# Attention and two expert layers on one core: the first batch's gate moves from TensorE's products into VectorE's row-maximum pass

## The chip, the cores and the metric

The kernel runs on one core of one Trainium2 chip. The metric is the device time of one execution in microseconds (us), the median of several executions. The engines have their usual names in the rows: PE is TensorE's matrix products and PEld its weight loads, DVE is VectorE, ACT is ScalarE, POOL is GpSimd, SP is the queue that issues most DMAs.

## The reference

The reference is a chain of three blocks in single precision. Only the first concerns the change: a causal attention over 4 batches, 8 heads, 576 positions and a head size of 64, whose scores get a gate from a running sum.

```python
scores = scale * np.matmul(q, k.transpose(0, 1, 3, 2))
s_pos = np.maximum(s, 0.0)
cum = np.cumsum(s_pos, axis=-1)
bias = -(cum[:, :, :, None] - cum[:, :, None, :])
scores = np.where(causal, -1000000000.0, scores + np.minimum(bias, 0.0))
scores = scores - np.max(scores, axis=-1, keepdims=True)
attn = np.exp(scores)
attn = attn / (np.sum(attn, axis=-1, keepdims=True) + 1e-09)
return np.matmul(attn, v).astype(np.float32)
```

Behind it stand a first expert layer (512 to 1024 to 512, softmax, normalization) and a second one (512 to 2048 to 512). The running sum never falls, so the minimum with 0 only acts above the diagonal, which the mask covers anyway. The part of the bias that belongs to the row (`-cum[i]`) is the same for all columns and drops out when the row's maximum is subtracted; only `+cum[j]` is left.

## The kernel before, in words

The 32 pairs of batch and head are worked two heads at a time. A head's rows are cut into five tiles (`SZ` = 128, 128, 128, 96, 96 rows, starting at `ST`), and tile `t` has only the columns up to its own end. Batches 1 to 3 hold q, k and the gate stacked along the contraction and split into high and low parts (`qk`, L615). The first batch is worked otherwise (`prep_whole`, `qk_whole`): q and k of a pair of heads are transposed in full precision (L445), head `j` on the partitions `64 j` to `64 j + 63`, and for every tile TensorE makes four products (L588), for each head one of the gate and one of q and k, which add up in one PSUM bank. The gate's product has contraction 64, of which 4 partitions are set: `gates_at` gives rows 0 to 3 of a zeroed block of `whole_t`, which hold the sum's high and low parts, once as such beside ones and once negated. These rows are made by `gate_rows` at the start: a running sum on VectorE (L283), three more VectorE instructions (L284 to L286), four stores to `rows_d` in DRAM (L290), and one load for each head (L432).

The first batch is worked in two ranges: first tiles 0 and 1 of all four pairs (`a=False`), whose output starts the first expert layer, then tiles 2 to 4 of all four pairs (`a=True`). For each product `tops` (L536) reads the bank and a causal mask, writes the negated score and gives the row's maximum in the same VectorE pass; ScalarE takes the exponential in place (L548); VectorE inverts the sums (L644, L645); GpSimd scales the rows (L649); TensorE transposes them (L683) and multiplies with v (L712). Between these stand the conversions of the expert weights from a 64-bit format: a load of 512 KB by ScalarE's queue (L322), instructions on ScalarE, VectorE (L332, L336, L343) and GpSimd (L352). The first expert layer starts with L799 and L803 (x into high and low parts) and its products L817.

No order is written by hand: the functions add operations to `Plan`, each with an engine, an assumed duration, the keys that it reads and writes, and for a DMA a `lag` until it has landed. `Plan.emit` plays these through and emits each engine's instructions in the order of the starts that come out. Engines run in that order; only real dependencies hold them.

`whole_t[0]` serves pairs 0 and 2, `whole_t[1]` pairs 1 and 3, of both ranges. For pairs 2 and 3 q and k lie in the same tile as the gate (`[:, :2]` and `[:, 2:4]`).

Of the kernel before, what the change touches and what calls it, by code (L numbers as in the profile page):

```python
# [18 lines left out]
NEG = -1.0e30  # L19
# [170 lines left out]
def kernel(ctx, tc, q, k, v, s, w_in, w_out, g_ln, w2_in, w2_out, out):  # L190
# [30 lines left out]
    rows_d = dram.tile([NH, 2, 4, S], F32, name="rows_d")  # L221
    x2_d = dram.tile([P, KDM, NT], F32, name="x2_d")
# [46 lines left out]
    def gate_rows():  # L269
# [3 lines left out]
        one = ap2.tile([P, S], F32, tag="y4", name="one")[:NH]  # L273
        cum = ap2.tile([P, NQ, 2, D], F32, tag="V", name="cum").rearrange("p c j d -> p (c j d)")[:NH, :S]
        pos = ap2.tile([P, PT_COLS], F32, tag="pt", name="pos", bufs=PT).bitcast(F32R)[:NH, : 2 * S]
        neg = ap2.tile([P, PT_COLS], F32, tag="pt", name="neg", bufs=PT).bitcast(F32R)[:NH, : 2 * S]
# [19 lines left out]
        plan.add("SP", 0.45, load, writes=["s"], lag=2.0)  # L296
        plan.add("DVE", 2.2, lambda: nc.vector.memset(one, 1.0), writes=["one"])
        for j in range(2):
            plan.add("POOL", 1.05, lambda j=j: zeros(j), writes=[f"zeros{j}"], new=[(f"stack{j}", 1, f"whole{j}")])
        plan.add("POOL", 0.4, constants)  # L300
# [3 lines left out]
        for i, r, src, key in ((1, 0, both(pos), "c"), (0, 1, both(neg), "c"), (0, 0, ones, "one"), (1, 1, ones, "one")):  # L304
# [228 lines left out]
    def tops(h, t, c0, c1, at, key):  # L533
# [3 lines left out]
            out=ys[h, t][:n, c0:c1], in0=bank(key)[:n, : c1 - c0], in1=mask[:n, 480 + n - w + c0 : 480 + n - w + c1], scale=-1.0, scalar=3.0e38,  # L537
# [20 lines left out]
    def qk_whole(p, t):  # L558
# [21 lines left out]
        def mm(c0, c1, keys):  # L580
            if c0 == 0:
                homes()
            for m in range(2):
                for j in range(2):
                    r = slice(j * D, (j + 1) * D)
                    g, hl = gates_at(p, j), hls[f"HL{p}"][r]
                    a, b = (hl[:, 0, :], hl[:, 1, :]) if m else (g[:, 0, :], g[:, 1, :])
                    nc.tensor.matmul(bank(keys[j])[:n, : c1 - c0], lhsT=a[:, ST[t] : w], rhs=b[:, c0:c1], start=(m == 0), stop=(m == 1))  # L588

        pieces = pieces_of(t)  # L590
        for c0, c1, at in pieces:
# [4 lines left out]
            elif c0 == 0 and t == ts[0]:  # L596
# [808 lines left out]
```

## Time and profile before

| | |
|---|---|
| median of 3 executions | 828.55 us (827.94 to 829.88) |
| profiled execution, first to last instruction | 826.7 us |
| PE busy in it | 800.2 us, 97% |
| DVE, ACT, POOL busy | 540.2 us, 424.0 us, 210.1 us |

The profiled execution has no time of its own beside its span. The median lies 1.85 us above that span and the fastest execution 1.2 us; what is read from the trace is a difference, and is taken from the median as it stands. All four engines work side by side, so their sums don't add up to the span; the engine's share says how much of it could be hidden behind another one.

### The profile page before, as it was taken

Reading aid. Unit: us, or ns where it says so; the run is one execution under the profiler, and the core shown is the slowest. Engines: PE = TensorE matmul, PEld = TensorE weight load, DVE = VectorE, ACT = ScalarE, POOL = GpSimd, SP = SyncE. Lnnn points to the kernel's source line nnn. Section 1 sums busy time; section 2 is a strip of 40 time slices with the busy share of each in tenths; the row PEclk is TensorE's granted clock in tenths of the full one; section 3 lists DMA queues with packets and bytes.
Section 4 is the critical chain, followed back from the end, with each engine's and each line's share of the span. In section 5 each row is a group of like instructions: output and inputs, shape, how many; then the busy total and the mean of one; then the engine's idle time right before and its main releaser. Section 6 shows DMA issues by size and latency. Waiting matters only on the chain.

```text
span 826.7 us, 14172 instructions
## 1 busy us (share of the span) xinstructions
PE 800.2 (97%) x4960; PEld 696.7 (84%) x4960; DVE 540.2 (65%) x1344; ACT 424.0 (51%) x994; POOL 210.1 (25%) x308
## 2 busy tenths in 40 slices
PE   3899999999999999999999999999999999999997
PEld 2655688898898888897999999999998989998996
DVE  3777887756847577648844994648867677455351
ACT  2575777756756566546644763335434335323223
POOL 2563653524632454245420231000000000000000
PEclk9999999999999999999999999999999999999999
DMA  6753586755645564305613679724424443524302
GB/s 167 192 155 105 124 212 142 175 134 130 132 99 137 138 131 99 89 27 172 192 52 111 221 217 355 261 78 135 172 101 145 161 140 134 210 90 147 121 1 76
DMA packets 110726, 117.41 MB, mean 142 GB/s; under 512 B 65248, under 2 KB 89312, under 8 KB 108608
## 3 DMA queue, kind: packets, MB, share of 16 engines
q1 hardware_dynamic: 108352, 108.12, 46.3%
q10 hardware_dynamic: 2304, 8.39, 3.1%
q8 instruction: 39, 0.64, 0.3%
q14 instruction: 31, 0.25, 0.1%
HBM read 68.45 MB, written 26.80 MB: 115 GB/s over the span
## 4 chain that ended last, share of the span: by engine, by line
PE 91%; DVE 4%; DMA 2%; POOL 2%; issue 1%; ACT 0%; POOLq 0%; SPq 0%; DVEq 0%; ACTq 0%
PE bank L1134 24%; PE bank L1270 14%; PE bank L904 12%; PE bank L817 11%; PE bank L1122 8%; PE bank L712 6%; PE bank L615 5%; PE bank L683 5%; PE bank L588 3%; PE bank L883 2%; PE bank L478 1%; DMA whole<-rows_d 1%; DMA rows_d<-neg 1%; POOL y L649 1%; POOL y L631 1%
## 5 line engine op out<-in xcount | busy, mean ns | idle before, releaser
L1134 PE MATMUL bank<-w2o,gb 128*128 128x512 f32 x576 | 137.2, 391 | 0.0
L1134 PEld LDWEIGHTS bank<-w2o,gb 128*128 128x128 f32 x576 | 107.6, 188 | 20.9
L1270 PE MATMUL bank<-xb,ws 128*128 128x384 f32 x672 | 123.8, 336 | 0.0
L1270 PEld LDWEIGHTS bank<-xb,ws 128*128 128x128 f32 x672 | 118.5, 188 | 3.2 <-DVE c L1283 0.3
L536 DVE CUSTOM_DVE_ANT_0 y<-bank,mask 96x288 f32<-96x288 f32 (+4 forms) x168 | 74.6, 467 | 57.0 <-PE bank L615 37.3
L548 ACT ACTIVATE y<-y,nmax 128x256 f32<-128x256 f32 (+4 forms) x140 | 83.5, 598 | 40.9 <-DVE nmax L536 27.7
L1283 DVE TENSOR_TENSOR c<-c,bank 128x384 f32<-128x384 f32 x112 | 60.3, 551 | 63.4 <-PE bank L1270 59.9
L631 POOL TENSOR_SCALAR y<-y,rsum 128x128 f32<-128x128 f32 (+4 forms) x120 | 68.9, 592 | 102.9 <-DVE rsum L627 42.5
L904 PE MATMUL bank<-zh,w_out_h 128*128 128x256 f32 x288 | 82.8, 288 | 0.0
L904 PE MATMUL bank<-zl,w_out_h 128*128 128x256 f32 x288 | 80.9, 281 | 0.0
L904 PE MATMUL bank<-zh,w_out_l 128*128 128x256 f32 x288 | 80.9, 281 | 0.0
L1122 PE MATMUL bank<-xk,wp 128*128 128x384 f32 x320 | 72.0, 337 | 0.0
L1134 PE MATMUL bank<-w2o,gs 128*128 128x512 f32 x288 | 71.7, 393 | 0.0
L1099 ACT ACTIVATE ggb<-c 128x384 f32<-128x384 f32 x64 | 32.7, 523 | 58.2 <-DVE c L1283 56.6
L817 PE MATMUL bank<-w_in_h,xh 128*128 128x512 f32 x144 | 61.4, 426 | 0.8 <-DVE xh L799 0.8
L1134 PEld LDWEIGHTS bank<-w2o,gs 128*128 128x128 f32 x288 | 53.6, 188 | 9.7
L1122 PEld LDWEIGHTS bank<-xk,wp 128*128 128x128 f32 x320 | 57.3, 188 | 1.9
L615 PE MATMUL bank<-stack 128*96 128x288 f32 (+4 forms) x288 | 57.8, 317 | 0.5 <-DMA stack<-rows_d 0.5
L817 PE MATMUL bank<-w_in_h,xl 128*128 128x512 f32 x144 | 57.3, 398 | 0.6 <-POOL xl L803 0.6
L817 PE MATMUL bank<-w_in_l,xh 128*128 128x512 f32 x144 | 57.2, 397 | 0.0
L904 PEld LDWEIGHTS bank<-zh,w_out_h 128*128 128x128 f32 x288 | 54.2, 188 | 1.1 <-DVE zl L890 0.2
L904 PEld LDWEIGHTS bank<-zh,w_out_l 128*128 128x128 f32 x288 | 54.3, 189 | 0.3
(239 smaller groups left out, 1521.6 us busy)
## 6 DMA issues: line engine op xcount, KB each, us to landing
ws<-ws_d SPq DMA_DIRECT2D x8, 1792.0 KB
raw_w2i<-in_moe_w_in_dram SPq DMA_DIRECT2D x16, 512.0 KB
raw_w2o<-in_moe_w_out_dram SPq DMA_DIRECT2D x16, 512.0 KB
ws<-ws_d SPq DMA_DIRECT2D x8, 1024.0 KB
ws_d<-ws SPq DMA_DIRECT2D x16, 512.0 KB
ws_d<-wp SPq DMA_DIRECT2D x24, 256.0 KB
rawq<-in_q_dram SPq DMA_DIRECT2D x32, 144.0 KB
rawk<-in_k_dram SPq DMA_DIRECT2D x32, 144.0 KB
```

The source lines that it names most:

```text
L536: nc.vector.tensor_tensor_reduce(out=ys[h, t][:n, c0:c1], in0=bank(key)[:n, : c1 - c0], in1=mask[:n, 480 + n - w + c0 : 480 + n - w + c1], ...
L548: nc.scalar.activation(out=y[:n], in_=y[:n], func=AF.Exp, bias=nmax[:n, h, t : t + 1], scale=-1.0, accum_out=sums[:n, h, t : t + 1])
L615: nc.tensor.matmul(bank(key)[:n, : c1 - c0], lhsT=ss[:, 2 - 2 * m, ST[t] : w], rhs=ss[:, 3 - 2 * m, c0:c1], start=(m == 0), stop=(m == 1))
L631: nc.gpsimd.tensor_scalar(ys[h, t][:n], ys[h, t][:n], rsum[:n, h, t : t + 1], 1.0, ALU.mult, ALU.mult)
L683: nc.tensor.transpose(bank(key)[: SZ[jj], c : c + SZ[t]], ys[h, t][: SZ[t], ST[jj] : ST[jj] + SZ[jj]], ident[: SZ[t], : SZ[t]])
L712: nc.tensor.matmul(bank(key)[j * D : (j + 1) * D, lo - c0 : c1 - c0], lhsT=vs[v_key(p, a)][:n, jj, j, :], rhs=pts[pt_key(2 * p + j, a)][:n ...
L817: nc.tensor.matmul(bank(key), lhsT=xs[i][m // 2][:, kk, :], rhs=(w_in_l if m == 1 else w_in_h)[:, kk, f * 512 : (f + 1) * 512], start=(kk ...
L904: nc.tensor.matmul(bank(key)[:, : 2 * P], lhsT=w_out_at(w, kk)[:, m * P : (m + 1) * P], rhs=z[:, kk, :], start=(kk == 0 and i == 0), stop= ...
L1122: nc.tensor.matmul(bank(key)[:, :W], lhsT=w2i_at(m, a)[:, c * P : (c + 1) * P], rhs=x[:, b, :], start=(c == 0 and i == 0), stop=(c == KDM ...
L1134: nc.tensor.matmul(bank(key), lhsT=g_t[name][:, i // 2, (t % TRIO) * P : (t % TRIO + 1) * P], rhs=w2o[m][:, i % 2, :], start=(m == 0 and i ...
L1270: nc.tensor.matmul(bank(key)[:, :W], lhsT=ws[bi, k][:, WOP[op], x, kc * P : (kc + 1) * P], rhs=xb[bi, op][:, y, kc, :], start=(kc == 0 and ...
L1283: nc.vector.tensor_add(g_t[to_key], g_t[from_key], bank(key)[:, :W])
```

## The change

In the first batch the gate no longer goes through TensorE. The running sum is stored once (`cum_d`, 72 KB) and for a pair and range one DMA reads the two heads' rows back to all 128 partitions (256 KB for tiles 0 and 1, 576 KB for tiles 2 to 4). GpSimd puts a large negative number above the diagonal of each tile's own block in this copy (`triangle`), and `tops` takes the copy in place of the mask. Since a tile's triangle spoils these columns for the tiles below it, tiles go from the last to the first of a range. The rows in `rows_d` are still made, for batches 1 to 3. The two zeroings of `whole_t` go. The planner is given new durations and keys. Cut to its core:

```diff
+    cum_d = dram.tile([NH, S], F32, name="cum_d")
...
-        plan.add("DVE", 3.0, sums, reads=["s", "one"], writes=["c"])
+        plan.add("DVE", 1.9, sums, reads=["s", "one"], writes=["c"])
...
+    def cum_store():
+        plan.add("SP", 0.4, lambda: nc.sync.dma_start(out=cum_d, in_=G["cum"]), reads=["c"], writes=["cumd"], lag=2.0)
...
-        def zeros(j):
-            whole_t[j] = ap1.tile([P, 4, S], F32, tag=f"stack{j}", name=f"whole{j}")
-            nc.gpsimd.memset(whole_t[j][:, 2:4, :], 0.0)
...
-    def gates_at(p, j):
-        return whole_t[p % 2][j * D : (j + 1) * D, 2:4, :]
...
     def load_gates(p, a):
+        n = S if a else CUT
         def gates():
-            for j in range(2):
-                nc.sync.dma_start(out=gates_at(p, j)[:4], in_=rows_d[2 * p + j].rearrange("i r s -> r i s"))
-        plan.add("SP", 0.8, gates, reads=ROWS_D + [f"zeros{p % 2}", f"whole{p % 2}"], writes=[f"G{p}{a}"], new=[("G", 2, f"G{p}{a}")], lag=2.0)
+            nc.sync.dma_start(out=whole_t[p % 2][:, 2:4, :n], in_=cum_d[2 * p : 2 * p + 2, :n].partition_broadcast(P))
+        plan.add("SP", 0.5, gates, reads=["cumd", f"zeros{p % 2}", f"whole{p % 2}"], writes=[f"G{p}{a:d}"], new=[("G", 2, f"G{p}{a:d}")], lag=2.0)
...
+    def triangle(p, a, j, t):
+        n = SZ[t]
+        def fill():
+            block = whole_t[p % 2][:n, 2 + j, ST[t] : ST[t] + n]
+            nc.gpsimd.affine_select(out=block, in_=block, pattern=[[-1, n]], compare_op=ALU.is_ge, fill=NEG, base=0, channel_multiplier=1)
+        plan.add("POOL", 0.4, fill, reads=[f"G{p}{a:d}"], writes=[gate_key(p, a, j, t)])
...
-    def tops(h, t, c0, c1, at, key):
+    def tops(h, t, c0, c1, at, key, rows=None):
...
-            out=ys[h, t][:n, c0:c1], in0=bank(key)[:n, : c1 - c0], in1=mask[:n, 480 + n - w + c0 : 480 + n - w + c1], scale=-1.0, scalar=3.0e38,
+            out=ys[h, t][:n, c0:c1], in0=bank(key)[:n, : c1 - c0], in1=mask[:n, 480 + n - w + c0 : 480 + n - w + c1] if rows is None else rows[:n, c0:c1], scale=-1.0, scalar=3.0e38,
...
-            for m in range(2):
-                for j in range(2):
-                    r = slice(j * D, (j + 1) * D)
-                    g, hl = gates_at(p, j), hls[f"HL{p}"][r]
-                    a, b = (hl[:, 0, :], hl[:, 1, :]) if m else (g[:, 0, :], g[:, 1, :])
-                    nc.tensor.matmul(bank(keys[j])[:n, : c1 - c0], lhsT=a[:, ST[t] : w], rhs=b[:, c0:c1], start=(m == 0), stop=(m == 1))
+            for j in range(2):
+                hl = hls[f"HL{p}"][j * D : (j + 1) * D]
+                nc.tensor.matmul(bank(keys[j])[:n, : c1 - c0], lhsT=hl[:, 0, ST[t] : w], rhs=hl[:, 1, c0:c1], start=True, stop=True)
...
-            qs = [(0.0013 * (ST[t] + SZ[t]), lambda p=p, t=t: qk_whole(p, t)) for t in ts]
+            qs = [(0.0013 * (ST[t] + SZ[t]), lambda p=p, t=t: qk_whole(p, t)) for t in reversed(ts)]
...
-    gate_rows()
+    cum_rows()
     load_qk(0)
+    cum_store()
...
     load_v(0, 0)
+    gate_rows()
```

What the planner makes of it stands in the orders. On PE at the start of the program, from the transposes of k of pair 0 on (`rawk`, `rawq` are the loaded k and q, `HL` the transposed ones, the number behind a name tells tiles apart), before:

```order
L445 MATMUL bank_93<-ident,rawk_118 128x96 x3
L445 MATMUL bank_94<-ident,rawk_118 128x96 x3
L588 MATMUL bank_95<-whole_111 128x128
L588 MATMUL bank_96<-whole_111 128x128
L588 MATMUL bank_95<-HL_140 128x128
L588 MATMUL bank_96<-HL_140 128x128
L445 MATMUL bank_97<-ident,rawq_150 128x96 x3
L445 MATMUL bank_98<-ident,rawq_150 128x96 x3
L588 MATMUL bank_91<-whole_111 128x256
L588 MATMUL bank_92<-whole_111 128x256
```

And with the change (L472 is the transpose, L613 the product):

```order
L472 MATMUL bank_94<-ident,rawk_128 128x96 x3
L472 MATMUL bank_95<-ident,rawk_128 128x96 x3
L613 MATMUL bank_96<-HL_139 128x256
L613 MATMUL bank_97<-HL_139 128x256
L613 MATMUL bank_98<-HL_139 128x128
L613 MATMUL bank_99<-HL_139 128x128
L472 MATMUL bank_92<-ident,rawq_147 128x96 x3
L472 MATMUL bank_93<-ident,rawq_147 128x96 x3
L472 MATMUL bank_94<-ident,rawk_168 128x96 x3
L472 MATMUL bank_95<-ident,rawk_168 128x96 x3
```

The products with `whole` are gone, and both tiles of pair 0 stand directly behind its transposes. In all of PE's order 48 products with `whole`'s gate are missing.

On the SP queue, from the stores of the ones on, before:

```order
L290 DMA rows_d<-one 32x2x576 x2
L290 DMA rows_d<-pos 32x2x576
L290 DMA rows_d<-neg 32x2x576
L400 DMA rawq_150<-in_q_dram 96x6x64 x2
L400 DMA rawk_165<-in_k_dram 96x6x64 x2
L432 DMA whole_111<-rows_d 4x2x576 x2
L418 DMA V0a<-in_v_dram 128x2x64
L984 DMA g_sb<-in_moe_g_ln_dram 128x8x1
L432 DMA whole_116<-rows_d 4x2x576 x2
```

And with the change:

```order
L313 DMA rows_d<-one 32x2x576 x2
L297 DMA cum_d<-cum 32x576
L414 DMA rawq_147<-in_q_dram 96x6x64 x2
L445 DMA whole_123<-cum_d 128x2x256
L414 DMA rawk_168<-in_k_dram 96x6x64 x2
L432 DMA V0a<-in_v_dram 128x2x64
L313 DMA rows_d<-pos 32x2x576
L313 DMA rows_d<-neg 32x2x576
L1014 DMA g_sb<-in_moe_g_ln_dram 128x8x1
L445 DMA whole_124<-cum_d 128x2x256
```

The gate's store now stands ahead of `pos` and `neg`, and its first load ahead of k of pair 1; the load of pair 1's gate stands behind `pos` and `neg`.

On DVE, where the first batch goes over from tiles 0 and 1 to tiles 2 to 4 (`yf` are the rows of pairs 1 and 3, `y_4` those of tile 4; the second instruction of each row maximum hands over its result), with the change:

```order
L563 ISA nmax 128x1
L563 ISA yf_402,nmax<-bank_92,whole_124 128x256
L563 ISA nmax 128x1
L350 SCALAR_TENSOR_TENSOR a_wi_1_426<-a_wi_1_426,t_wi_1_415 128x512
L672 TENSOR_SCALAR rsum<-sums 128x2x2
L673 RECIPROCAL rsum<-rsum 128x2x2
L563 ISA yf_401,nmax<-bank_95,whole_124 128x128
L563 ISA nmax 128x1
L563 ISA yf_402,nmax<-bank_96,whole_124 128x128
L563 ISA nmax 128x1
L346 TENSOR_SCALAR t_wi_1_450<-raw_wi_1_411 128x512
L563 ISA y_4_446,nmax<-bank_93,whole_123 96x288
```

And before, at the same turn:

```order
L536 ISA yf_393,nmax<-bank_97,mask 128x256
L536 ISA nmax 128x1
L332 TENSOR_SCALAR t_wi_1_428<-raw_wi_1_374 128x512
L719 COPY x_340<-bank_92 128x256
L336 SCALAR_TENSOR_TENSOR a_wi_1_426<-a_wi_1_426,t_wi_1_428 128x512
L536 ISA yf_394,nmax<-bank_95,mask 128x256
L536 ISA nmax 128x1
L536 ISA y_3_362,nmax<-bank_93,mask 96x480
L536 ISA nmax 96x1
L332 TENSOR_SCALAR t_wi_1_453<-raw_wi_1_411 128x512
L536 ISA y_4_368,nmax<-bank_94,mask 96x288
```

The row maximum of tile 4 of pair 0 now reads `whole_123`, which pair 2's last row maximum gives free; that one stands four instructions ahead of the first one shown, so 14 stand between. Before, it read the mask, and tile 3 came first.

## Rows read from the trace of the kernel before

**Rows 1.** The page's first part: each engine's busy time and share.

```profile
PE 800.2 (97%) x4960; PEld 696.7 (84%) x4960; DVE 540.2 (65%) x1344; ACT 424.0 (51%) x994; POOL 210.1 (25%) x308
```

**Rows 2.** Windows: busy time of each engine by stretch, then granted clock, DMA, GB/s.

```profile
0.00:24.00 24.00, 11.07 (x57) 8.29 (x58) 10.51 (x29) 6.26 (x19) 6.38 (x13) 1.00 0.75 178
24.00:55.00 31.00, 25.89 (x184) 16.46 (x184) 22.23 (x76) 20.65 (x60) 16.63 (x22) 1.00 0.56 156
55.00:95.00 40.00, 37.99 (x233) 24.32 (x234) 31.40 (x92) 25.89 (x61) 22.34 (x29) 0.96 0.50 131
95.00:112.00 17.00, 16.86 (x137) 13.19 (x136) 15.39 (x49) 12.93 (x34) 8.06 (x12) 1.00 0.63 148
```

**Rows 3.** The chain that ended last, its start: start us, us, what.

```profile
0.72 1.86 DMA s_sb<-in_s_dram
...
3.11 1.36 DVE cum L283
...
7.21 5.51 DMA rows_d<-neg
...
12.78 2.42 DMA whole<-rows_d
```

**Rows 4.** Timeline of DVE: first row maximum of pair 0, last of pair 1.

```profile
16.62 0.29 DVE L536 CUSTOM_DVE_ANT_0 y<-bank,mask 128x128 f32<-128x128 f32 x1 [4.66 <-PE bank L588]
...
24.33 0.42 DVE L536 CUSTOM_DVE_ANT_0 yf<-bank,mask 128x256 f32<-128x256 f32 x1
```

**Rows 5.** Timeline of PE, products of pair 1, tiles 0 and 1.

```profile
21.02 0.80 PE L588 MATMUL bank<-whole 64*128 64x128 f32 x4
21.61 0.64 PE L588 MATMUL bank<-HL 64*128 64x128 f32 x4
22.04 1.06 PE L588 MATMUL bank<-whole 64*128 64x256 f32 x4
22.89 1.06 PE L588 MATMUL bank<-HL 64*128 64x256 f32 x4
```

**Rows 6.** Timeline of PE, products of pair 1, tiles 2 and 3.

```profile
42.94 0.92 PE L588 MATMUL bank<-whole 64*128 64x384 f32 x4
43.69 0.81 PE L588 MATMUL bank<-HL 64*128 64x384 f32 x4
44.33 0.97 PE L588 MATMUL bank<-whole 64*96 64x480 f32 x4
45.14 0.97 PE L588 MATMUL bank<-HL 64*96 64x480 f32 x4
```

**Rows 7.** Windows, instructions of L588 alone: PE, PEld, clock, DMA, GB/s.

```profile
0.00:60.00 60.00, 21.46 (x128) 13.22 (x128) 0.97 0.67 169
60.00:95.00 35.00, 11.44 (x64) 4.95 (x64) 1.00 0.44 120
```

**Rows 8.** Groups of POOL's instructions by line: busy us, mean ns.

```profile
L294 POOL MEMSET whole<- 128x1152 f32 x2 | 2.1, 1058 | 0.3 <-POOLq L1389 0.3
...
masks.py:199 POOL TENSOR_SCALAR_AFFINE_SELECT ident<-ident 128x128 f32<-128x128 f32 x1 | 1.2, 1250 | 0.1
...
L267 POOL TENSOR_SCALAR_AFFINE_SELECT mask<-mask 128x128 f32<-128x128 f32 x1 | 0.4, 388 | 0.1
```

**Rows 9.** The chain that ended last, at the turn to tiles 2 to 4.

```profile
28.90 3.91 DMA whole<-rows_d
```

**Rows 10.** Timeline of DVE and of POOL around 54 us.

```profile
54.04 1.42 DVE L332 TENSOR_SCALAR t_wi<-raw_wi 128x512 int32<-128x512 uint32 x1
53.90 1.28 POOL L803 TENSOR_TENSOR xl<-x,xh 128x512 fp32r<-128x512 f32 x1 [2.98 <-DVE rsum L644]
```

**Rows 11.** Groups of DVE's instructions by line, up to 95 us.

```profile
L332 DVE TENSOR_SCALAR t_wi<-raw_wi 128x512 int32<-128x512 uint32 x8 | 4.7, 582 | 2.7 <-DMA raw_wi<-in_moe_w_in_dram 2.7
```

**Rows 12.** Timeline of PE: the first product of the first expert layer.

```profile
53.87 0.50 PE L817 MATMUL bank<-w_in_h,xh 128*128 128x512 f32 x1 [0.80 <-DVE xh L799]
```

**Rows 13.** Windows: the stretch behind it, all engines, then granted clock.

```profile
56.00:58.00 2.00, 2.00 (x6) 1.59 (x5) 2.00 (x13) 1.36 (x4) 2.00 (x4) 0.50 1.28 254
```

More of the change, by code (lines that the diff above doesn't have):

```diff
@@ L267, in constants, with cum_rows @@
         nc.gpsimd.affine_select(out=mask[:, 480:], in_=mask[:, 480:], pattern=[[-1, P]], compare_op=ALU.is_ge, fill=NEG, base=0, channel_multiplier=1)
-    def gate_rows():
+    G = {}
+    def cum_rows():
         s_sb = ap2.tile([P, S], F32, tag="y4", name="s_sb")[:NH]
[L273 to L276, printed above, removed]
+        G["one"] = one = ap2.tile([P, S], F32, tag="y4", name="one")[:NH]
+        G["cum"] = cum = ap2.tile([P, NQ, 2, D], F32, tag="V", name="cum").rearrange("p c j d -> p (c j d)")[:NH, :S]
         def load():
@@ L283, in sums, with home, gate_rows, split @@
             nc.vector.tensor_tensor_scan(cum, one, s_sb, 0.0, ALU.mult, ALU.add)
+        def home(j):
+            whole_t[j] = ap1.tile([P, 4, S], F32, tag=f"stack{j}", name=f"whole{j}")
+        plan.add("SP", 0.45, load, writes=["s"], lag=2.0)
+        plan.add("DVE", 0.6, lambda: nc.vector.memset(one, 1.0), writes=["one"])
+        for j in range(2):
+            plan.add("SP", 0.0, lambda j=j: home(j), writes=[f"zeros{j}"], new=[(f"stack{j}", 1, f"whole{j}")])
+        plan.add("POOL", 0.4, constants)
+        plan.add("DVE", 1.9, sums, reads=["s", "one"], writes=["c"])
+    def cum_store():
+        plan.add("SP", 0.4, lambda: nc.sync.dma_start(out=cum_d, in_=G["cum"]), reads=["c"], writes=["cumd"], lag=2.0)
+    def gate_rows():
+        one, cum = G["one"], G["cum"]
+        pos = ap2.tile([P, PT_COLS], F32, tag="pt", name="pos", bufs=PT).bitcast(F32R)[:NH, : 2 * S]
+        neg = ap2.tile([P, PT_COLS], F32, tag="pt", name="neg", bufs=PT).bitcast(F32R)[:NH, : 2 * S]
+        def split():
             nc.vector.tensor_copy(pos[:, :S], cum)
@@ L290, in put @@
             nc.sync.dma_start(out=dst, in_=src)
-        def zeros(j):
-            whole_t[j] = ap1.tile([P, 4, S], F32, tag=f"stack{j}", name=f"whole{j}")
-            nc.gpsimd.memset(whole_t[j][:, 2:4, :], 0.0)
-        plan.add("SP", 0.45, load, writes=["s"], lag=2.0)
-        plan.add("DVE", 2.2, lambda: nc.vector.memset(one, 1.0), writes=["one"])
-        for j in range(2):
-            plan.add("POOL", 1.05, lambda j=j: zeros(j), writes=[f"zeros{j}"], new=[(f"stack{j}", 1, f"whole{j}")])
-        plan.add("POOL", 0.4, constants)
-        plan.add("DVE", 3.0, sums, reads=["s", "one"], writes=["c"])
+        plan.add("DVE", 2.6, split, reads=["c"], writes=["cs"])
         ones = one.unsqueeze(1).to_broadcast([NH, 2, S])
         both = lambda c: c.bitcast(F32).rearrange("p (i s) -> p i s", i=2)
-        for i, r, src, key in ((1, 0, both(pos), "c"), (0, 1, both(neg), "c"), (0, 0, ones, "one"), (1, 1, ones, "one")):
+        for i, r, src, key in ((1, 0, both(pos), "cs"), (0, 1, both(neg), "cs"), (0, 0, ones, "one"), (1, 1, ones, "one")):
             plan.add("SP", 0.55, lambda i=i, r=r, src=src: put(i, r, src), reads=[key], writes=[f"rows/{i}{r}"], lag=2.0)
@@ L563, in qk_whole @@
         ts = [i for i in range(NQ) if (ST[i] >= CUT) == late]
+        first = t == ts[-1]
         def homes():
@@ L568, in homes @@
                     ys[h, t] = ap2.tile([P, w], F32, tag=f"y{t}", name=f"y{h}_{t}")
-                elif t == ts[0]:
+                elif first:
                     cols = sum(ST[i] + SZ[i] for i in ts)
@@ L582, in mm @@
                 homes()
[L583 to L588 removed]
+            for j in range(2):
+                hl = hls[f"HL{p}"][j * D : (j + 1) * D]
+                nc.tensor.matmul(bank(keys[j])[:n, : c1 - c0], lhsT=hl[:, 0, ST[t] : w], rhs=hl[:, 1, c0:c1], start=True, stop=True)
+        for j in range(2):
+            triangle(p, late, j, t)
         pieces = pieces_of(t)
```

13 lines of the change are left out of this document (8 added, 5 removed).

## The prediction

> **What bounds the kernel now.** I read the page's busy times first [rows 1]: PE works 800.2 of 826.7 us, so 26.5 us are idle, and a shorter PE is worth something wherever PE is what is waited for. The windows [rows 2] say where that is. Up to 112 us PE is busy 91.8 of 112 (11.07 + 25.89 + 37.99 + 16.86), so 20.2 of the 26.5 idle us lie there; 12.9 of them before 24 us, 5.1 from 24 to 55, 2.0 from 55 to 95. After that PE is full. The first batch's scores, all that the change touches, lie before 95 us. There are thus three regimes: a start in which PE waits, a stretch to 55 us in which it is full five sixths of the time, and from 55 us on one in which it sets the pace.
>
> The chain of waits [rows 3] explains the start. The running sum is there at 4.47 us; three more VectorE instructions make the split rows, the store of `neg` takes from 7.21 to 12.72, the load of the gate rows from 12.78 to 15.20, and only then does the first product start. The first row maximum starts at 16.62, the last one of pairs 0 and 1 ends at 24.75 [rows 4].
>
> At the same time VectorE is not idle. From 24 to 112 us it is busy 69.0 of 88 us (22.23 + 31.40 + 15.39), a share of 0.78, and 0.91 in the last 17 us [rows 2]. Whoever takes work from PE there must ask whether VectorE follows.
>
> **What the change removes.** Of each tile's two pairs of products one goes, 48 products in all. Their price is the distance from the start of the gate's products to the start of those with q and k, since ends overlap. At full speed [rows 6]: 0.75 us for 384 columns, 0.81 for 480. The two 288-column pieces of tile 4 lie between 0.49 (480's rate) and 0.75; I take 0.55. So tiles 2 to 4 of a pair give 0.75 + 0.81 + 2 x 0.55 = 2.66, four pairs 10.6. Tiles 0 and 1 of pair 1 gave 0.59 and 0.85 [rows 5], 1.44; the 256 columns take as long as 480 do later, so PE ran at half speed there. Pairs 0 and 1 together 2.9, pairs 2 and 3 at half of that price 1.4. Sum 14.9 us; half of all L588 work in the windows [rows 7] is (21.46 + 11.44)/2 = 16.4, with overlapping ends counted. One third of it (11.44 of 32.90), 5.2 us, lies after 60 us, where PE sets the pace; 9.7 us lie earlier.
>
> Two zeroings of 1.06 us each go from GpSimd [rows 8]. They stand ahead of the identity that the first transposes need. Earlier transposes bring nothing as long as the row maxima wait for the gate (below), so I count nothing.
>
> **What it adds.** (1) *The way of the gate at the start.* The sum is stored at once, then read back. The store of 72 KB lies between 1.86 us (72 KB of `s`) and 5.51 (`neg`, 144 KB) [rows 3]; I take 2.9, since the two stores of ones stand ahead of it on SP's queue and the weights' loads not yet. The read-back of 256 KB lies between 2.42 us (two loads of 18 KB, rows 3) and 5.51; q of pair 1 and 1 MB of weights share the engines then, and I take 4.2. A triangle is priced by the mask's of the same 128 x 128, 0.39 us [rows 8]; the identity's took 1.25, the upper bound, and 96/128 of 0.39 is the lower one. So the first row maximum comes at 4.5 + 2.9 + 4.2 + 0.4 + 0.3 of hand-overs = 12.3 instead of 16.6 (bounds 9.4 and 17.1). By then both tiles' products of pair 0 have long stood in their banks. Pair 1's read-back stands behind `pos` and `neg` on SP: I put it 4 us behind the first, so that row maxima of pair 1 end about 18.0 where they ended at 24.75. **Lead at that point: 6.7 us** (bounds 1.9 and 9.6).
>
> (2) *Waits in the middle.* From 24.75 to the first expert product at 53.87 [rows 12] the work passes through all engines, and the read-backs for tiles 2 to 4 are 576 KB where 36 KB went. Even these 36 KB took 3.91 us [rows 9]. In VectorE's order 14 instructions stand between the row maximum that frees the buffer and the one that needs the first of them: four row maxima of 0.29 to 0.42 us [rows 4], 1.4 in all, and three copies or conversions, at 0.58 [rows 11] 1.7; the rest is small. That is some 3.1 us of work. Landing and triangle take at least 3.91 + 0.4 = 4.3, at most 5.51 + 1.25 = 6.8: VectorE waits 1.2 to 3.7 us there, and behind it stand the conversions of weights, whose GpSimd step waits in turn. The second read-back follows on the same queue. I take 2.0 us lost in all (0 to 6). What PE saves before 55 us, 9.7 us, is no second gain: it is how the lead arises.
>
> (3) *GpSimd.* 40 triangles, at 0.39 us 15.6 us, in a stretch where it was busy 45.4 of 95 us [rows 2]: room enough. But its reads hold VectorE up: the conversion at 54.04 took 1.42 us, ending with GpSimd's subtraction [rows 10], against 0.58 in the mean [rows 11]. About 20 such conversions and copies in 95 us; GpSimd's share rises by (15.6 - 2.1)/95 = 0.14, a hit costs 0.2 on average: 0.6 us, I take 0.5 (0 to 20 x 0.39 = 7.8). The Trainium skill, "SBUF — State Buffer", section "Who interferes with whom", says that VectorE's two-port modes and GpSimd share one pair of ports under an exclusive lock, and whoever comes second is blocked for the whole instruction. The row agrees; by that rule alone the 7.8 would be the ceiling, which only a hit every time reaches.
>
> (4) *The row maximum itself.* It reads a bank and one row in SBUF, as before; same shapes, nothing added.
>
> (5) *From 55 us.* PE loses 5.2 us of work and VectorE none. VectorE at 0.78 has room up to 95 us, little in the last 17: I let 0.4 go.
>
> **Sum.** 6.7 - 2.0 - 0.5 + 5.2 - 0.4 = 9.0 us off the span, 817.7; off the median 819.5. It asks little of VectorE: 69.5 us of work in about 86 us instead of 69.0 in 88, a share of 0.81.
>
> **Rivals.** *All of it is kept.* PE's 14.9 us come off whole and no new wait costs anything; for it speaks that after 112 us PE hardly waits, against it that PE was idle 18 us of the first 55. Time 813.6, with the lead's upper bound, 2.9 us more, 810.7.
>
> *VectorE sets the pace.* Its share stays 0.78 from 24 us on; then only the lead less the waits and hits is kept, 4.2 us: 824.3. For it the 0.91 before 112 us, against it the idle VectorE that waited for PE's L588 (16.62's 4.66 us, rows 4).
>
> *PE's clock.* With half its products gone PE has more gaps early. Its matmuls ran at half speed up to 24 us, as the 256 columns show, and after a gap of 0.80 us before the first expert product [rows 12] the granted clock fell to 0.50, the 1.2 GHz level, from 56 to 58 us [rows 13]. If it stayed low to 40 us of the old time, the work left from 24 to 40 us (at 25.89 of 31 [rows 2] 13.4 us, less some 3 of gate products) would take 10 us more, of which the gaps, 2.6 us of before and the 3 of products, absorb less than 6: some 4 to 5 us are lost at least, I take 6. Gain 3, time 825.5. The Trainium skill, "TensorE: Matmul & The Clock Gate", part 1, puts it so: "the default state is throttled, and activity releases the throttle"; by that rule alone taking work from PE can slow the rest. The window agrees that the clock falls after gaps.
>
> *Slower: the read-back holds VectorE.* Each of the six later read-backs stands before a row maximum at the head of VectorE's queue, and everything behind it waits. Without such waits the gain is 6.7 + 5.2 - 0.9 = 11.0; 11.0/6 = 1.8 us for each is the point from which it decides. At 2.45, the middle of the 1.2 to 3.7 above, it is 6 x 2.45 = 14.7, slower by 3.7: 832.3. For it the 3.91 us of a tiny load, against it that the read-backs of pairs 2 and 3 have tens of instructions between release and use.
>
> **Chances and range.** Forecast (7 to 12 us less) 0.45; all kept (12 to 17) 0.17; VectorE's pace (2 to 7) 0.18; clock (0 to 5) 0.08; slower 0.09; no effect 0.03. A measurement of this kernel tells about 0.2%, 1.7 us. Faster: 0.45 + 0.17 + 0.17 + 0.05 = 0.84; same 0.07; slower 0.09. From 811 (all kept and the longest lead) to 827 leaves out the slower case, part of those without effect, and a tail of the second: about 0.15.
>
> **What would show it.** Right: first row maximum near 12.3 us, last of pair 1 near 18; first expert product near 49.7; L588's successor at about half of 32.9 us of PE; the same PE work after 112 us, shifted by 9. Wrong: VectorE idle before row maxima with the DMA or a triangle as releaser for more than 3 us in sum (waits too cheap); PE idle between 55 and 112 us above 4 us with VectorE as releaser (its pace); matmuls at double length past 24 us or a granted clock of 0.50 for longer than before (the clock). The step I trust least is the 2.0 us of waits.

## The result, and the profile after

The changed kernel takes 840.6 us (838.93 to 842.87) where the kernel before, measured beside it, takes 829.05 (827.94 to 829.88): ratio 1.0138, 95% interval [1.0115, 1.0161]. It is 1.4% slower; 819.5 was forecast.

The page of the changed kernel, busy time of each engine, against [rows 1]:

```profile
span 839.9 us, 14070 instructions
...
PE 797.6 (95%) x4864; PEld 694.1 (83%) x4864; DVE 543.0 (65%) x1344; ACT 426.0 (51%) x994; POOL 217.1 (26%) x346
```

PE has 96 matmuls fewer (48 products, two records each) but only 2.6 us less to do, and the span is 13.2 us longer: PE is idle for 42.3 us instead of 26.5. The windows of the changed kernel, columns as in [rows 2], say where:

```profile
0.00:24.00 24.00, 8.90 (x46) 7.18 (x47) 10.92 (x29) 7.13 (x21) 5.90 (x20) 1.00 0.85 194
24.00:55.00 31.00, 23.74 (x118) 14.37 (x118) 19.34 (x64) 15.28 (x43) 18.89 (x36) 0.94 0.72 199
55.00:95.00 40.00, 34.47 (x196) 22.06 (x195) 33.84 (x92) 25.80 (x64) 25.82 (x42) 0.91 0.50 146
95.00:112.00 17.00, 12.67 (x92) 9.21 (x91) 15.13 (x46) 13.85 (x36) 10.06 (x17) 0.93 0.69 144
112.00:160.00 48.00, 44.31 (x328) 36.68 (x327) 35.41 (x117) 31.24 (x83) 19.38 (x33) 0.99 0.71 162
```

Idle are 15.1, 7.3, 5.5, 4.3 and 3.7 us, 35.9 in 160; before it was 20.9. The granted clock is below full speed in four of the five stretches. The start is not what the prediction saw either; SP's timeline of the changed kernel (start us, us to issue, line, what):

```profile
4.49 0.31 SPq L297 DMA_DIRECT2D cum_d<-cum  x1
5.99 0.87 SPq L414 DMA_DIRECT2D rawq<-in_q_dram  x2
6.96 0.45 SPq L445 DMA_DIRECT2D whole<-cum_d  x1
7.52 2.53 SPq L414 DMA_DIRECT2D rawk<-in_k_dram  x2
10.10 2.30 SPq L432 DMA_DIRECT2D V0a<-in_v_dram  x1
12.51 2.27 SPq L313 DMA_DIRECT2D rows_d<-pos  x1
```

and GpSimd's, PE's and VectorE's:

```profile
15.99 0.54 POOL L459 TENSOR_SCALAR_AFFINE_SELECT whole<-whole 128x128 f32<-128x128 f32 x2 [13.57 <-DMA whole<-cum_d]
...
33.11 0.29 POOL L459 TENSOR_SCALAR_AFFINE_SELECT whole<-whole 128x128 f32<-128x128 f32 x1 [7.35 <-DMA whole<-cum_d]
...
15.48 1.20 PE L472 MATMUL bank<-ident,rawq 96*128 96x96 f32 x6 [6.57 <-DMA rawq<-in_q_dram]
...
57.83 0.50 PE L845 MATMUL bank<-w_in_h,xh 128*128 128x512 f32 x1 [0.47 <-DVE nmax L563]
...
16.32 0.42 DVE L563 CUSTOM_DVE_ANT_0 y<-bank,whole 128x256 f32<-128x256 f32 x1 [8.72 <-POOL whole L459]
...
25.79 0.29 DVE L563 CUSTOM_DVE_ANT_0 yf<-bank,whole 128x128 f32<-128x128 f32 x1
```

The first read-back is issued at 6.96 and ready at 15.99. The way to the first triangle is 9.0 us, where 4.2 were forecast; and q of pair 1, issued just ahead of it, reaches PE only at 15.48. The next three rows on SP take over 2 us each. So the first row maximum comes at 16.32 (16.62 before), the last one of pair 1 ends at 26.08 (24.75 before), the first expert product comes at 57.83 (53.87 before). The lead never arose. Among the largest waits, by the view of waits up to 160 us, are these (engine, line, releaser: us in total, times, longest):

```profile
POOL whole L459 <- DMA whole<-cum_d: 30.0, 4, 13.6
...
PE bank L472 <- DMA rawq<-in_q_dram: 17.1, 4, 6.6
...
DVE y L563 <- POOL whole L459: 8.7, 1, 8.7
```

These rows invite the story that the loss is the engines' standing behind the read-back, each in its order. The experiments were made to test it, and it falls.

### The profile page after: what moved, and what is told of

Its sections match the earlier page's. It is cut to its first block, busy times and chain, and to the rows that moved or that the text cites. A ratio compares the mean times of both kernels' runs of the same rounds, so it can differ in the third digit from the quotient of the medians.

```text
span 839.9 us, 14070 instructions
## 1 busy us (share of the span) xinstructions
PE 797.6 (95%) x4864; PEld 694.1 (83%) x4864; DVE 543.0 (65%) x1344; ACT 426.0 (51%) x994; POOL 217.1 (26%) x346
## 4 chain that ended last, share of the span: by engine, by line
PE 86%; DMA 4%; DVE 4%; issue 3%; POOL 2%; ACT 0%; POOLq 0%; ACTq 0%; DVEq 0%
PE bank L1164 24%; PE bank L1300 14%; PE bank L932 12%; PE bank L845 10%; PE bank L1152 8%; PE bank L740 5%; PE bank L711 5%; PE bank L643 5%; PE bank L911 2%; DMA whole<-cum_d 1%; PE bank L505 1%; PE bank L613 1%; DMA raw_wo<-in_moe_w_out_dram 1%; DMA stack<-HL12k 1%; DMA stack<-HL6k 1%
## 5 line engine op out<-in xcount | busy, mean ns | idle before, releaser
L1164 PEld LDWEIGHTS bank<-w2o,gb 128*128 128x128 f32 x576 | 107.6, 188 | 20.9
L575 ACT ACTIVATE y<-y,nmax 128x384 f32<-128x384 f32 (+4 forms) x140 | 83.4, 597 | 49.3 <-DVE nmax L563 40.4
L659 POOL TENSOR_SCALAR y<-y,rsum 128x128 f32<-128x128 f32 (+4 forms) x120 | 67.2, 580 | 125.2 <-DVE rsum L655 62.7
L563 DVE CUSTOM_DVE_ANT_0 y<-bank,mask 96x288 f32<-96x288 f32 (+2 forms) x144 | 63.9, 466 | 45.8 <-PE bank L643 41.7
L711 PE MATMUL bank<-ident,y 96*128 96x96 f32 (+2 forms) x420 | 55.5, 267 | 9.3 <-DVE pt0b L715 3.7
L711 PEld LDWEIGHTS bank<-ident,y 96*128 96x128 f32 (+2 forms) x420 | 45.7, 143 | 16.6 <-POOL y L677 4.4
```

The lines of the kernel that those rows point to most:

```text
L563: nc.vector.tensor_tensor_reduce(out=ys[h, t][:n, c0:c1], in0=bank(key)[:n, : c1 - c0], in1=mask[:n, 480 + n - w + c0 : 480 + n - w + c1] ...
L575: nc.scalar.activation(out=y[:n], in_=y[:n], func=AF.Exp, bias=nmax[:n, h, t : t + 1], scale=-1.0, accum_out=sums[:n, h, t : t + 1])
L659: nc.gpsimd.tensor_scalar(ys[h, t][:n], ys[h, t][:n], rsum[:n, h, t : t + 1], 1.0, ALU.mult, ALU.mult)
L711: nc.tensor.transpose(bank(key)[: SZ[jj], c : c + SZ[t]], ys[h, t][: SZ[t], ST[jj] : ST[jj] + SZ[jj]], ident[: SZ[t], : SZ[t]])
L1164: nc.tensor.matmul(bank(key), lhsT=g_t[name][:, i // 2, (t % TRIO) * P : (t % TRIO + 1) * P], rhs=w2o[m][:, i % 2, :], start=(m == 0 and i ...
```

## The experiments

Every ratio is to the kernel before. "PE idle" is worked out from the windows of one profiled execution: its first 160 us, and of these the last 65. It need not be a typical one: in twice and all_free_small it is the shortest, 5.0 and 5.3 us under the median, in maxima_free the longest, 3.5 us over it. So these two columns are not to be compared to the microsecond.

| run | median us | ratio to before, 95% | PE idle 0 to 160 | 95 to 160 |
|---|---|---|---|---|
| before | 829 to 830 | 1 | 20.9 | 0.8 |
| the change | 840.6 | 1.0138 [1.0115, 1.0161] | 35.9 | 8.0 |
| no_products | 824.1 | 0.9937 [0.9919, 0.9955] | 23.4 | 0.8 |
| small_read | 834.0 | 1.0064 [1.0042, 1.0086] | 29.1 | 7.5 |
| no_triangle | 841.4 | 1.0139 [1.0106, 1.0173] | 34.9 | 6.5 |
| twice | 845.0 | 1.0169 [1.0135, 1.0204] | 27.0 | 6.3 |
| wide | 827.1 | 0.9977 [0.9963, 0.9992] | 23.8 | 0.8 |
| old_order | 829.4 | 1.0006 [0.9994, 1.0018] | 25.3 | 2.2 |
| lag6 | 834.7 | 1.0061 [1.0040, 1.0081] | 31.3 | 4.9 |
| hybrid | 836.9 | 1.0093 [1.0064, 1.0123] | 28.9 | 1.1 |
| old_order_reversed | 838.3 | 1.0110 [1.0093, 1.0126] | 33.2 | 4.1 |
| no_products_reversed | 824.9 | 0.9945 [0.9923, 0.9967] | 24.0 | 2.4 |
| start_of_before | 832.7 | 1.0046 [1.0025, 1.0068] | 28.7 | 1.4 |
| pe_cost | 842.5 | 1.0147 [1.0123, 1.0171] | 35.9 | 6.5 |
| maxima_free | 837.3 | 1.0102 [1.0074, 1.0130] | 37.2 | 8.8 |
| all_free | 840.4 | 1.0125 [1.0097, 1.0154] | 37.6 | 9.0 |
| start_lag6 | 830.0 | 1.0013 [1.0001, 1.0024] | 30.8 | 2.2 |
| hybrid_reversed | 831.0 | 1.0024 [1.0011, 1.0037] | 24.4 | 3.3 |
| all_free_small | 836.2 | 1.0087 [1.0067, 1.0107] | 28.8 | 4.7 |
| all_free_start | 831.4 | 1.0025 [1.0016, 1.0035] | 29.5 | 1.1 |

**What each part is worth by itself.** no_products, from before:

```diff
-            for m in range(2):
...
-                    nc.tensor.matmul(bank(keys[j])[:n, : c1 - c0], lhsT=a[:, ST[t] : w], rhs=b[:, c0:c1], start=(m == 0), stop=(m == 1))
+                    nc.tensor.matmul(bank(keys[j])[:n, : c1 - c0], lhsT=hl[:, 0, ST[t] : w], rhs=hl[:, 1, c0:c1], start=True, stop=True)
```

> The kernel before without the gate's products (first batch's gate left out, all loads and the order kept). If what went wrong is only what the change adds (read-backs or triangles), this gains most of PE's 14.9 us: 813 to 821 us. If TensorE's clock suffers from the missing products themselves, the gain is under 4 us: 825 or more, with products of tiles 0 and 1 still at half speed past 30 us.

Gain 5.2 us (0.63%), of 14.9 forecast for the products; the time, 824.1, lies between the two ranges. Its PE waits up to 200 us begin with

```profile
PE bank L445 <- DMA rawq<-in_q_dram: 12.7, 3, 6.4
```

where before's begin with the gate rows, 9.4 us: PE now waits for q, which reaches it at 14.43 for pair 1. PE's busy time falls by 9.0 us (791.2) and idle time rises by 2.6 up to 160 us. Its first expert product comes at 50.38, near the forecast 49.7.

small_read, from the change:

```diff
+            nc.gpsimd.memset(whole_t[j][:, 2:4, :], 0.0)
...
-            nc.sync.dma_start(out=whole_t[p % 2][:, 2:4, :n], in_=cum_d[2 * p : 2 * p + 2, :n].partition_broadcast(P))
+            nc.sync.dma_start(out=whole_t[p % 2][:4, 2:4, :n], in_=cum_d[2 * p : 2 * p + 2, :n].partition_broadcast(4))
```

> The changed kernel, same order, with each read-back going to 4 partitions instead of 128 (the gate is left out for all other rows; two zeroings at the start for the rest). Theory of the transfers (3.3 MB of read-backs fill the DMA engines and come late, with the loads of q and k): 840.6 falls to 822 or less, and q of pair 1 lands before 11 us instead of 15.5. Theory of the clock and theory of the triangles: it stays at 835 or more.

6.1 us come back, but it is still 0.64% slower than before; 834.0 lies between the two ranges. q of pair 1 reaches PE only at 14.62, hardly later than in no_products and 0.9 us earlier than in the change: what makes q late is for the most part not the read-back's size.

no_triangle, from the change, in the same order:

```diff
-            nc.gpsimd.affine_select(out=block, in_=block, pattern=[[-1, n]], ...)
+            pass
```

> The changed kernel, same order, without the 40 triangles (the first batch's scores above the diagonal are not masked). Theory of the triangles (GpSimd stands before a read-back in its queue, weights' conversions and row scaling wait behind it): 826 or less. Theory of the transfers: not more than 4 us come off, 836 or more, as VectorE waits for the same read-backs itself.

twice, from the change, in the same order:

```diff
+            for _ in range(2):
-            for j in range(2):
+                for j in range(2):
```

> The changed kernel, same order, with every product of q and k of the first batch made twice, so that TensorE has the work of before. Theory of the clock (half speed costs more than the work saved): 836 or less in spite of 15 us more work. Theory of the transfers: 841 to 850, as PE idles early and only what lies after 55 us, some 5 us, is added.

The triangles cost nothing that can be measured. Filling PE again brings nothing: in the profile of twice PE is idle 9 us less than in the change up to 160 us, and pays it with work. So the clock is not the net cause.

**Volume and order.** wide, from no_products:

```diff
-            for j in range(2):
-                nc.sync.dma_start(out=gates_at(p, j)[:4], in_=rows_d[2 * p + j].rearrange("i r s -> r i s"))
+            n = S if a else CUT
+            nc.sync.dma_start(out=whole_t[p % 2][:, 2:4, :n], in_=rows_d[2 * p : 2 * p + 2, 1, 0, :n].partition_broadcast(P))
```

> The kernel no_products (before with the gate's products of the first batch left out and nothing put in their place, so that the gate is missing from that batch; 824.1 us) with one edit: its eight gate loads bring one stored row of each head to all 128 partitions (256 and 576 KB) in place of 4 to 4 partitions. Nothing reads them, and every engine's instructions stand in the same order. If the transfers' volume alone is what costs (6.8 us between the change and small_read), 829 to 832 us, with q of pairs 1 to 3 landing 2 us or more later than in no_products. If it costs only where the row maxima wait for it, or only in the changed order, 824 to 825.

It costs 3.3 us (0.40%), between the two ranges: the smaller part. The window of wide shows the transfers (DMA share 0.99 and 250 GB/s, against 0.77 and 186 in no_products):

```profile
24.00:55.00 31.00, 27.01 (x140) 15.94 (x139) 23.15 (x82) 20.85 (x59) 17.35 (x24) 0.83 0.99 250
```

old_order, from no_products: wide's read-back from a stored sum, triangles, and rows for `tops`, with the planner's numbers and places of before. The order that comes out is not quite the one of before: on PE the two kernels' orders agree again only from some 170 us on. Tiles ascend, so a tile's triangle also covers columns that tiles below it still read.

```diff
+        plan.add("SP", 0.4, lambda: nc.sync.dma_start(out=cum_d, in_=cum), reads=["c"], writes=["cumd"], lag=2.0)
...
+        for j in range(2):
+            triangle(p, late, j, t)
...
-... tops(h, t, c0, c1, at, key), reads=[key],
+... tops(h, t, c0, c1, at, key, whole_t[p % 2][:, 2 + j, :]), reads=[key, f"G{p}{late:d}", ...]
```

> The whole change (store, read-backs to all partitions, triangles, row maxima that add the row, no gate products) in the order of before: tiles ascending, planner's costs and places of before, running sums and both splits together at the start, one store more behind the rows' stores. If the new order is what the rest of the loss comes from (some 4.5 us that the volume does not explain), about that of wide, 829 to 834 us; if it is the row maxima's wait for the read-backs, as slow as the changed kernel, 838 to 842.

It is 0.06% above before, 1.32% below the change with the same transfers, triangles and waits. lag6:

```diff
-...writes=["cumd"], lag=2.0)
+...writes=["cumd"], lag=4.0)
-...new=[("G", 2, f"G{p}{a:d}")], lag=2.0)
+...new=[("G", 2, f"G{p}{a:d}")], lag=6.0)
```

> The changed kernel, but the planner counts 6.0 us from a read-back's issue to its landing and 4.0 us for the store, in place of 2.0, about what the trace of the changed kernel shows (3.4 to 7.0), so that it places the waiting work later. If the loss is that VectorE, GpSimd and ScalarE stand in order behind work whose data the planner thinks has landed, 3 to 6 us come back: 835 to 838. If it is the volume and the late q loads, 840 to 842.

It gives back 0.77%; 834.7 is just under the range for the waits. hybrid is before with the change under `if late:` (read-back, triangle, row in `tops`, one product); tiles ascend here too, with the same consequence.

> Before, with the change in tiles 2 to 4 alone: tiles 0 and 1 keep the gate's products and their rows, so the first four read-backs (256 KB each, in the stretch where q and k land late) are gone, and the four late ones of 576 KB stay; tiles ascending. If the early read-backs and the start are where the loss is: the late products' part of 5.4 us back less what is left of the volume, 825 to 828 us. If the volume costs wherever it falls (2.4 of the 3.4 MB are here): 829 to 831.

A miss: 836.9, slower than old_order, which has more transfers and, in tiles 2 to 4, the same waits. This speaks for the order, but doesn't show it. Its idle time lies elsewhere than the change's: 7.8 us from 55 to 95 us (2.0 before), and 1.1 from 95 to 160.

**Which part of the order.** old_order_reversed and no_products_reversed have the same edit:

```diff
-... for t in ts]
+... for t in reversed(ts)]
```

> The kernel old_order (829.4 us) with one edit: the tiles of a pair run from the last to the first, as in the changed kernel, so that a triangle is written only when no other tile still reads its block. If the reversed order makes the loss, 836 us or more; if it is the start of the changed kernel (store and read-back ahead of the first q and k, the splits later) or its planner's costs, 828 to 832. If the planner's order turns on any small thing, anything between.

> The kernel no_products (before with the gate's products of the first batch left out and nothing in their place; 824.1 us) with the tiles of a pair from the last to the first, as in the changed kernel: no transfer, wait or operation is added. If the reversed order is bad by itself, 830 us or more; if it only matters where row maxima wait for the read-back, 823 to 826.

The reversal costs 1.04% in the one, with 9.2 us of PE idle from 55 to 95 us, and 0.08%, nothing that can be told, in the other. start_of_before, from the change:

```diff
     cum_rows()
+    gate_rows()
+    cum_store()
     load_qk(0)
-    cum_store()
...
     load_v(0, 0)
-    gate_rows()
```

> The changed kernel, but both splits and the rows' stores are written ahead of the first q and k loads again, and the sums' store behind them, as in before. If the loss is made at the start (q of pair 1 behind the first read-back on SP's queue), 830 to 834 us; if it is the reversed order or the waits of the row maxima, 838 to 842.

It gives back 0.92%, though the tiles stay reversed. pe_cost puts `4 * max(0.07, 0.00033 * (c1 - c0))` for PE's `0.1 + 0.00167 * (c1 - c0)`:

> The changed kernel with one edit in the planner: two products of 256 columns count 0.34 us, the formula of before, in place of 0.53. It moves some 50 rows of TensorE's order and 4 of the loads. If the order is good or bad by such small things, this moves the time by 3 us or more either way; if the loss comes from transfers and waits that every order of the change has, 839 to 842.

No difference that can be told.

**The waits.** maxima_free has the first of these edits, all_free both; the order of every engine and queue is kept:

```diff
-... tops(h, t, c0, c1, at, key, whole_t[p % 2][:, 2 + j, :]),
+... tops(h, t, c0, c1, at, key),
...
-            nc.gpsimd.affine_select(out=block, in_=block, pattern=[[-1, n]], ...)
+            pass
```

> The changed kernel with one edit: the row maxima of the first batch's first 40 tiles add the constant mask, as before, not the row read back (so the gate is missing from that batch). The read-backs and the triangles still run, and every engine's instructions stand in the same order; only VectorE's wait for the read-back is gone, GpSimd's (triangles) stays. If the loss is that VectorE stands behind the read-back, 829 to 833 us; if GpSimd's wait is enough, or the order alone is bad, 838 to 841.

> maxima_free with the triangles left out as well: the read-backs run, in the same order of every queue, and nobody waits for them (again without the gate in the first batch). What stays of the loss against no_products (824.1) is the volume (some 3 us by the kernel wide) and the order. If waiting behind the read-back in two engines' queues is the loss, 827 to 831; if the order itself is bad, 836 or more.

This decides against the waits. In all_free nobody waits for a read-back, and the time stays: 840.4. (maxima_free, 837.3, lies between its two ranges, 0.36% below the change; the intervals overlap.) VectorE's timeline of all_free shows the row maxima freed:

```profile
8.89 0.42 DVE L563 CUSTOM_DVE_ANT_0 y<-bank,mask 128x256 f32<-128x256 f32 x1 [1.02 <-PE bank L613]
...
23.23 0.28 DVE L563 CUSTOM_DVE_ANT_0 yf<-bank,mask 128x128 f32<-128x128 f32 x1
```

Pair 1 ends at 23.51, and the first expert product comes within 0.02 us of before:

```profile
53.85 0.50 PE L845 MATMUL bank<-w_in_h,xh 128*128 128x512 f32 x1 [0.47 <-DVE nmax L563]
```

The loss is behind it; windows of all_free:

```profile
95.00:112.00 17.00, 14.48 (x91) 9.89 (x89) 11.44 (x35) 9.96 (x27) 8.41 (x13) 0.76 0.49 106
112.00:160.00 48.00, 41.54 (x310) 34.84 (x307) 33.23 (x111) 30.13 (x79) 17.64 (x31) 1.00 0.76 160
```

and the same of no_products:

```profile
95.00:112.00 17.00, 16.20 (x126) 13.53 (x125) 14.56 (x45) 12.72 (x32) 9.00 (x10) 1.00 0.80 196
112.00:160.00 48.00, 48.00 (x383) 41.55 (x382) 38.15 (x131) 36.53 (x101) 22.36 (x40) 1.00 0.76 169
```

9.0 us of PE idle against 0.8, at the turn to the second batch (HL5 and HL6 below are two of its pairs). The waits of PE in all_free from 95 to 160 us:

```profile
PE bank L643 <- DMA stack<-HL5k: 2.9, 1, 2.9
PE bank L643 <- DMA stack<-HL6q: 2.6, 1, 2.6
PE bank L711 <- POOL yl L677: 2.5, 2, 1.5
```

These are loads and scalings of work that the change doesn't touch, in the place that the planner gave them.

Where the loss ends can be read too. By the names of the matmuls PE's order is the same before and with the change from one product of the second expert layer on, in the timelines of PE before and with the change:

```profile
169.60 0.36 PE L904 MATMUL bank<-zh,w_out_h 128*128 128x256 f32 x1
...
182.38 0.36 PE L932 MATMUL bank<-zh,w_out_h 128*128 128x256 f32 x1
```

It comes 12.8 us later, and the span is 13.2 us longer: nearly all of the loss is made where the orders differ.

start_lag6 joins the edits of start_of_before and lag6; hybrid_reversed is hybrid with late tiles reversed, two products counted as two and lag 6.0.

> start_of_before (832.7 us) and the planner's 6.0 us for a read-back and 4.0 for the store together, the whole change and nothing left out. If both edits do the same thing, getting other work ahead of the waits, 831 to 834; if they add up, 826 to 829.

> hybrid (836.9 us; before, with the change in tiles 2 to 4 alone) with those tiles from the last to the first, so that nothing is left out, 6.0 us for the late read-backs in the planner and two products of a tile counted as two. If the planner's wrong numbers are what made hybrid slow, 827 to 831; if four late read-backs of 576 KB and their waits cost whatever the order, 834 to 838.

start_lag6, 830.0, lies between its two ranges. These are two orders in which all of the change, or its late part, is as good as free: 0.13% and 0.24% slower than before. No kernel that computes everything beats before.

**Two orders by two volumes, nobody waiting.** all_free_small is all_free with small_read's edit, all_free_start is all_free with that of start_of_before.

> all_free (the changed kernel's order, nobody waits for a read-back; 840.4 us) with the eight read-backs cut to 4 partitions, all queues in the same order, again without the gate in the first batch. With no_products (824.1), wide (827.1) and all_free it makes two orders by two volumes, without waits. If the changed order costs by itself, 832 to 836; if it costs only because the large read-backs stand ahead of the loads, 824 to 828.

> all_free with one edit, that of start_of_before: splits and rows' stores written ahead of the first q and k loads, the sums' store behind them; the large read-backs run and nobody waits for them. If the start of the order is what costs, 828 to 832, near start_of_before (832.7), whose row maxima do wait; if its gain came from shorter waits behind the read-back, 837 to 841.

| | 4 partitions | 128 partitions |
|---|---|---|
| order by the plan of before | 0.9937 (no_products) | 0.9977 (wide) |
| order of the change | 1.0087 (all_free_small) | 1.0125 (all_free) |

The order costs 0.0150 and 0.0148, 12.4 and 12.3 us of 829.5; the volume 0.0040 and 0.0038, 3.3 and 3.2 us. The second volume step lies within the two intervals. Within a row of this table every engine's work stands in the same order (wide has one load where no_products has two). What the lower row has beside its order, the sum's store of 72 KB and no zeroings, is counted with the order. The four executions of all_free_small spread from 831.0 to 838.1, and the profiled one (span 829.2) is the shortest.

## Why the prediction was wrong

Taken one after the other (no_products, wide, all_free) the measured parts are: products -5.2, volume +3.3, order +12.3, together +10.4; the change measured +11.4, so that waits, triangles and what the intervals can't tell have 1 us.

- **"Lead at that point: 6.7 us" failed**, in its term for the way of the gate: store and read-back were given 2.9 + 4.2 us; from the store's issue at 4.49 to the first triangle at 15.99 it took 11.5. The bound of 5.51 for a read-back, taken from a store of 144 KB, was too low: the first took 9.0 to its first use, pair 2's 7.0 (25.99 to 32.99) to its landing. Of the other six the trace gives one landing, 3.4 us after its issue. The prediction named q of pair 1 as sharing the engines, and did not ask when q itself would land: in every run in which PE stands idle for it, it comes at 13.8 to 15.9 us, and pair 1 can't be earlier. But this was not what decided: all_free doesn't wait for a read-back, and no_products, where q comes at 14.43, has the first expert product 3.5 us earlier than before (50.38) and gains 5.2 us in the end.
- **The step from the lead to the end of the span failed.** All_free reaches the first expert product as early as before and takes 1.25%, 10.4 us, longer; all_free_start reaches it 4.5 us later than all_free and takes 1.00%, 8.3 us, less (profiled spans 827.8 and 839.0); no_products_reversed reaches it 8.1 us later than no_products and takes the same time. How early that product comes doesn't tell the time. PE's timelines show it in no_products, no_products_reversed and all_free_start:

```profile
50.38 0.50 PE L814 MATMUL bank<-w_in_h,xh 128*128 128x512 f32 x1 [0.93 <-DVE xh L796]
...
58.46 0.78 PE L814 MATMUL bank<-w_in_h,xh 128*128 128x512 f32 x1
...
58.35 0.50 PE L845 MATMUL bank<-w_in_h,xh 128*128 128x512 f32 x1 [0.97 <-DVE nmax L563]
```

  The prediction assumed "the same PE work after 112 us, shifted by 9". In the changed kernel 8.0 us of PE idle lie after 95 us, where the kernel before has 0.8.
- **What was left out: the planner re-orders everything.** The prediction read two or three places of the order and priced the instructions there. The change gave the planner other durations, keys and places in the code, and it moved SP's loads and PE's work up to the start of the third batch, some 165 us into the kernel before. One part, where `gate_rows` and `cum_store` stand in the code, is worth 0.92% with the waits and 1.00% without. The planner's 2.0 us for the store and for a read-back, where one read-back took 7.0 to its landing and another 3.4, is worth 0.77%. Both together 1.25% of 1.38%: they overlap. The slower side thus had a cause that was none of the rivals.
- **"Waits in the middle", 2.0 us (0 to 6): the mechanism is there, the price nil.** VectorE did wait for read-backs (2.00 us at 47.58 in the changed kernel) and GpSimd 30.0 us in 4 times, but all_free against the change is 1.0125 to 1.0138. The price holds for this order: start_of_before, with waits, and all_free_start, without, in one order, are 1.0046 and 1.0025 with overlapping intervals; old_order is 0.29% above wide, clear of the intervals, but its order differs from wide's too, so that waits and order can't be told apart there. The rival *slower: the read-back holds VectorE* ended on the right side, 832.3, by the wrong mechanism. The sign named for it, over 3 us of VectorE's idle time before row maxima, stood in the trace (8.72 us) and would have led astray: a long wait in a row is no price until the kernel has run without it.
- **PE's 5.2 us after 60 us and the 14.9 in all.** The work went: L613 takes 13.80 us up to 60 and 7.00 to 95, 20.8 in all, where half of [rows 7] is 16.4. So 12.1 us went, not 14.9: what is left costs more than half. The granted clock doesn't explain it, for in no_products, with the clock of before in both stretches, the same products (L585) take 14.72 and 6.71, 21.4 in all; why stays open. The windows of L613 with the change, and of L585:

```profile
0.00:60.00 60.00, 13.80 (x60) 8.15 (x60) 0.97 0.79 200
60.00:95.00 35.00, 7.00 (x36) 2.65 (x36) 0.90 0.44 134
...
0.00:60.00 60.00, 14.72 (x64) 6.52 (x64) 0.97 0.73 177
60.00:95.00 35.00, 6.71 (x32) 2.27 (x32) 1.00 0.51 126
```

- **The rival of PE's clock** was right on the row and wrong on the sum. The same 4864 matmuls take 797.6 us in the change and 791.2 in no_products; 6.4 us more PE time, in one execution each, and the change's granted clock is the lower one from 55 to 160 us; against that stand 12.5 us more idle up to 160 us. That the clock follows the gaps is not shown: twice gives PE its work back and has fewer gaps than the change, but its granted clock reads 0.79 and 0.83 in the first two stretches, where the change has 1.00 and 0.94. The Trainium skill, "TensorE: Matmul & The Clock Gate", part 1, says that activity releases the throttle; these rows of twice don't bear it out, and no run here settles it.

```profile
0.00:24.00 24.00, 11.80 (x64) 9.79 (x65) 9.92 (x28) 6.78 (x20) 6.33 (x21) 0.79 0.81 197
24.00:55.00 31.00, 25.15 (x161) 16.11 (x162) 20.80 (x68) 17.60 (x49) 19.84 (x37) 0.83 0.76 214
```

- **GpSimd's hits on VectorE, 0.5 us, and VectorE's pace, 0.4.** Triangles took 13.4 us, 0.35 us each; leaving them out changed nothing (no_triangle), so that the price of 0.39 was near and hits on VectorE are not seen in the time. The row that they were read from was weak: the conversion at 54.04 ends at 55.46, 0.28 us behind GpSimd's subtraction and not with it [rows 10]. VectorE is busy 114.7 of 160 us; it did not set the pace.

What stays open: which moved instruction makes the idle time from 95 to 160 us, or from 55 to 95 us in hybrid and old_order_reversed. The start, the lag and (in old_order) the direction of the tiles each move it, no one of them alone, and none of these runs puts one instruction back. Of the volume it is shown that it costs 3.3 us in the order of before; in the order of the change that lies within the intervals.

## What to carry to other kernels

Where a planner sets the order, a change is two: the work, and a new order of everything. Measure them apart, by a kernel that keeps the order and takes out one thing, before a wait in the trace is called the cause; and run the same change under two or three orders, since here these span 11 us (old_order 829.4, the change 840.6), twice what the removed work is worth. Give the planner the landing times that the trace shows.

## What was not expected of the hardware

- In the changed kernel a read-back of 256 KB took 9.0 us from its issue to its first use, and another, for pair 2, 7.0 to its landing; of q's loads of 144 KB the trace gives two landings up to 60 us, 2.7 and 9.0 us after the issue. The Trainium skill, "DMA: Bandwidth & Descriptors", section "Anatomy of one DMA — SWDGE (gpsimd) path", gives a fit of 2.0 us and the bytes at 436 GB/s for DMAs issued by GpSimd, an estimate of 2.6 us for 256 KB. These were issued by SP among other loads, and the first took over three times as long.
- While these run, three rows of SP's own issues take 2.27 to 2.53 us, where the stretch's other ones take 0.31 to 0.87 (the rows of SP above): the queue that issues is held, not only the data. The size of the read-back is not what holds it: in small_read, where 4 partitions are read back, the issue of V0a at 9.80 takes 2.48.
- PE's matmuls ran at about half speed in the first window, though its granted clock reads 1.00: six transposes of one shape take 1.20 us at 15.48 (above) and 0.66 later in the changed kernel's timeline:

```profile
104.72 0.66 PE L505 MATMUL bank<-ident,rawq 96*128 96x96 f32 x6
```
